# The way back of the 48-point stage: four frequencies in three packed matrix products

## The chip, the cores and the metric

One core of a Trainium2 chip runs one program. The metric is the device time of the program in microseconds (us), as the median of the runs shown. Engines: TensorE (PE; its weight loads PEld), VectorE (DVE), ScalarE (ACT), GpSimd (POOL), SyncE (SP, which here issues nearly all DMAs).

## The reference

The first half is a long convolution of 8 sequences (B = 8, S = 5696, D = 128) with one filter, along the sequence, by a real Fourier transform of length 2S. The second half is a mixture of experts with one expert of eight for each of the 45568 tokens:

```python
Xf = np.fft.rfft(x, n=L, axis=1); Hf = np.fft.rfft(h, n=L, axis=0)
y = np.fft.irfft(Xf * Hf[None], n=L, axis=1)[:, :S, :]
...
logits = x @ w_gate
expert_idx = np.argmax(logits, axis=1)
...
    h = np.maximum(xe @ w1[e], 0.0)
    ye = h @ w2[e]
    out[mask] = gate_w[mask, None] * ye
```

All inputs and outputs are float32.

## The kernel before

The transform of length 2 x 48 x 119 is cut into a 119-point stage and a 48-point stage. The batch is cut into three groups of 2, 3 and 3 sequences (`SPLIT`, line 40). For each group there are three phases. Phase A (`steps_a`, line 285) is the 119-point stage and writes its spectrum to memory in device DRAM. Phase B (`phase_b`, line 458) reads it by frequency, q = 0 to 119, transforms 48 points, multiplies with the filter's spectrum, transforms 48 points back and writes to DRAM. Phase C (`phase_c`, line 728) does the way back of the 119-point stage, finds each token's expert, and scatters the tokens, sorted by expert, to DRAM. A pipeline of expert tiles of 256 tokens (`pipeline`, line 1332) runs beside the later phases: an expert step is a quarter of a tile, first layer (`layer1`, line 1211), relu (line 1224) and second layer (`layer2`, line 1240).

The program order of every engine is written by hand: `run` (line 1418) merges streams (the phases, the preparation of expert weights, the expert pipeline) by costs that each stream yields. Phase B yields 0.45 of an expert step for a frequency of group 1 and 0.85 for group 2 (`MIX_B`, line 53, used in line 669); the preparation of weights (`weights`, line 258) is a third stream that lies beside group 1. Engines work through their own queues in that order and wait for each other by semaphores.

In phase B of groups 1 and 2 a step n treats one frequency of 3 x 128 = 384 columns (QW = 1); four frequencies (QB = 4, a block) share one load and one store. In step n, in this order:

- loads are issued for blocks to come: `load_m`, `load` (lines 631 to 634)
- stores that are `HOLD` = 3 steps old are issued on SP (line 645)
- `forward(n)`, line 537: one product of 96 rows with a 96 x 128 matrix into a bank of PSUM (tag `cx`, 4 banks in turn)
- `inverse(n - 4)`, line 574: one product of the 128 rows of `zt` with a 128 x 96 matrix (line 581) into the next `cx` bank, of which 96 partitions are used
- `product(n - 1)`, line 548: three VectorE operations (lines 557, 562, 564) that read the forward product's bank and write `zt` and `xs`
- `combine(n - 2)`, line 569: a sum on POOL (line 572; while the last sorts of group 2 run, on VectorE)
- `save(n - 5)`, line 590: ScalarE copies 96 partitions of the bank to `vt` (line 596); after the fourth, one store of the block is queued

The lags 1, 2, 4 and 5 are `BLAGS` (line 38). `zt` has 4 - 1 + 2 = 5 buffers (line 553). Each float32 product shows in the trace as two matmul records with a weight load each. The expert step of tiles 18 and later (`PLAIN`) works in split precision: six records for each of the two layers, and a remainder that VectorE forms (line 1234). Before that tile a layer has four float32 records and no remainder; the remainder of the weights is formed by VectorE in the preparation (line 279).

Column strips are in use before: `logit` (line 815) places products of 32 result rows side by side with `tile_position` (line 819), and `synth` in groups 1 and 2 puts two of 64 rows side by side (line 780). A table of tiles is made by `tables` (line 1029), which takes a `cx` bank too (line 1086); the guest is phase A of the next group, run inside phase C two halves a step (`Guest`, line 359, called in line 951).

Of the kernel before, what the change touches and what calls it, by code (L numbers as in the profile page):

```python
# [13 lines left out]
F32 = mybir.dt.float32  # L14
# [9 lines left out]
NB = 48  # L24
MB = 119
QN = 2 * 60
MP = 128
HQ = 60
HM = 64
# [12 lines left out]
SIX = 4  # L42
# [20 lines left out]
HOLD = 3  # L63
# [16 lines left out]
def conv_moe(ctx: ExitStack, tc: tile.TileContext, I, out, B, S, D, E, F, split):  # L80
    nc = tc.nc
    P = 128
    K2 = 2 * NB
# [6 lines left out]
    def pool(name, bufs, space=None):  # L90
        kw = {} if space is None else {"space": space}
        return ctx.enter_context(tc.tile_pool(name=name, bufs=bufs, **kw))
# [4 lines left out]
    ps = pool("ps", 2, PSUM)  # L97
# [15 lines left out]
    sb = Space()  # L113
# [21 lines left out]
    class Group:  # L135
        def __init__(self, g, b0, nb):
# [13 lines left out]
            self.qb = 4 if self.cols <= 384 else (3 if self.cols <= 512 else 2)  # L150
            rows = dram.tile([2 * QN + 2 * PR, NB, self.cols], F32, name=f"VU{g}")
            self.U = [rows[2 * QN + k * PR : 2 * QN + (k + 1) * PR] for k in range(2)]
            self.V = rows
# [4 lines left out]
    for g, nb in enumerate(split):  # L158
        gr = Group(g, b0, nb)
        gr.parts = []  # L160
        for upto in HALVES[g]:
            rows = sum(MB - (i + (MB - 1) * NB >= S) for i in range(upto * gr.ni))
            sure = max(0, (b0 * S + nb * rows - E * (T - 1) + T - 1) // T)
            tiles = (total if b0 + nb == B and upto * gr.ni == NB else sure) - done
# [6 lines left out]
    def by_frequency(gr, q, count, out):  # L171
        lo = 2 * (q % HQ)
        if out:
            rows = gr.V[2 * q : 2 * (q + count)]
        else:
            rows = gr.U[q // HQ][lo : lo + 2 * count]
        return rows.rearrange("(q c) i x -> (c i) q x", c=2)

    for pt in parts[:-1]:
        pt.filled = True  # L180
    HS = dram.tile([QN // 4, NB, 2, 4, D], F32, name="HS")
    WD = dram.tile([4, E * P, F], F32, name="WD")

    fcs = const.tile([MP, 3, PR], F32, name="c_fcs")
    nc.sync.dma_start(fcs, I["fcs"])
    half = fcs[:, 2]
    uht = sb.tile([K2, QN, D], F32, tag="uht", name="uht", bufs=1)
    sb.open("a")
    fcr = const.tile([MP, 2, 2, PR], F32R, name="fcr")
    nc.vector.tensor_copy(fcr[:, 0], fcs[:, :2])  # L190
# [14 lines left out]

    gcs = part_of(2 * MP, QN).rearrange("p (k m) -> p k m", k=2)
    wg = part_of(32)
    wt9 = part_of(2 * E1, MP).rearrange("p (c e) -> p c e", c=2)
    where = part_of(NB * B, MP).bitcast(I32).rearrange("p (i b) -> p i b", b=B)
    base0 = part_of(E1)  # L210
    lane = part_of(2).bitcast(I32)
    lt = part_of(MP // 2, MP).bitcast(BF16)
    upto = part_of(E * E, E)
# [188 lines left out]
    def phase_h():  # L402
# [26 lines left out]
        for n in range(nd + 2):  # L429
            cut(n + 1)  # L430
            if n < nd:
                hc = hcs.pop(n).rearrange("p v i d -> p v (i d)")
                for c in range(2):
                    banks[c] = ps.tile([P, 512], F32, tag="mh", name=f"ph{n}_{c}", bufs=2)
                    for k, (u, v) in enumerate(PASSES):
                        nc.tensor.matmul(
                            banks[c][:QN, : NB * W], fcr[:, u, c, :QN], hc[:, v], start=(k == 0), stop=(k == 2)
                        )
# [19 lines left out]
    def phase_b(gr, guest=None):  # L458
        g, cb, cw, nch, QB, QW = gr.g, gr.cb, gr.cw, gr.nch, gr.qb, gr.qw
        dp, dc, di, ds_ = BLAGS[g]  # L460
        tiles, outs_ = {}, {}
# [36 lines left out]

        mats, hhs, hbank = {}, {}, {}
        zts, banks, late, clock = {}, {}, [], [0]  # L500

        def back(qb):
            if g or qb * QB >= QN:
# [44 lines left out]
        def product(n):  # L548
            q, c = items[n]
            qb, k0 = divmod(q, QB)  # L550
            hh = hhs[qb]
            xs = sb.tile([P, cb, QW * D], F32, tag="xs", name=f"xs{g}_{q}_{c}", bufs=dc - dp + 2)
            zt = sb.tile([P, cb, QW * D], F32, tag="zt", name=f"zt{g}_{q}_{c}", bufs=di - dp + 2)
            x3 = banks.pop(n)[:, : QW * cw].rearrange("p (b x) -> p b x", b=cb)
            hv = hh[:, :, k0 : k0 + QW].rearrange("p c j (o d) -> p c o (j d)", o=1)
            wide = [cb, QW * D]
            nc.vector.tensor_tensor(out=zt, in0=x3, in1=hv[:, 0].broadcast_to([P] + wide), op=ALU.mult)  # L557
            for k in range(2):
                at, to = slice(k * HP, (k + 1) * HP), slice((1 - k) * HP, (2 - k) * HP)
                him = hv[at, 1].broadcast_to([HP] + wide)  # L560
                if k == 0:
                    nc.vector.tensor_tensor(out=xs[to], in0=x3[at], in1=him, op=ALU.mult)  # L562
                else:
                    nc.vector.scalar_tensor_tensor(  # L564
                        out=xs[to], in0=x3[at], scalar=-1.0, in1=him, op0=ALU.mult, op1=ALU.mult
                    )
            zts[n] = (zt, xs)
# [6 lines left out]
        def inverse(n):  # L574
# [12 lines left out]
                )  # L587
            banks[n] = vp

        def save(n):  # L590
            q, c = items[n]
            qb, k0 = divmod(q, QB)
            if k0 == 0 and c == 0:
                outs_[qb] = sb.tile([K2, QB, gr.cols], F32, tag="six", name=f"vt{g}_{q}", bufs=SIX)
            dst = outs_[qb][:, k0 : k0 + QW, c * cw : (c + 1) * cw]
            nc.scalar.copy(dst, banks.pop(n)[:K2, : QW * cw].rearrange("p (j x) -> p j x", x=cw))  # L596
            if k0 + QW == QB and c == nch - 1:
                late.append((clock[0], by_frequency(gr, qb * QB, QB, True), outs_.pop(qb)))
                tiles.pop(qb), hhs.pop(qb), mats.pop(qb)

        items = [(q, c) for q in range(0, QN, QW) for c in range(nch)]
        per = QB // QW * nch
        N = len(items)
        deep = 4 if g == 0 else 2
# [20 lines left out]
                filt(qb, k)  # L625
        for m in range(4 if g == 0 else 0):
            filt_save(0, m)
        for n in range(N + ds_ + 2 + (HOLD if QW == 1 else 0)):
            qb, k0 = divmod(n, per)
            clock[0] = n  # L630
            if k0 == (0 if g == 0 else 1):
                load_m(qb + deep)
            if k0 == (0 if g == 0 else min(3, per - 1)):
                load(qb + 2)
            if g == 0:
                if n < N:
                    forward(n)
                for k in range(QB // per):
                    filt(qb + 2, k0 * (QB // per) + k)
                for m in range(4 // per):  # L640
                    filt_save(qb + 1, k0 * (4 // per) + m)
                if k0 == 0:
                    back(qb)
            while late and late[0][0] <= n - (HOLD if QW == 1 else 1):
                nc.sync.dma_start(*late.pop(0)[1:])
            if n < N and g:
                forward(n)
            if 0 <= n - di < N:
                inverse(n - di)
            if 0 <= n - dp < N:  # L650
                product(n - dp)
            if 0 <= n - dc < N:
                combine(n - dc)
            if 0 <= n - ds_ < N:
                save(n - ds_)
                while late and g == 0 and n >= N:
                    nc.sync.dma_start(*late.pop(0)[1:])
            if k0 == 0:
                back_save(qb)
            if k0 == (0 if per == 1 else per - 1):  # L660
                twin(qb + 1)
            if n == 0:
                twin(0)
            drained = guest if n >= N + di - 1 and g in GUESTED else None
            if n == N - 4 and g in FETCHED and guest:
                guest.fetch()
            if drained:
                drained.begin(2)
            yield max(cw * 7 / 2.4 + 200, 2 * cw / 0.96 + 300) * QW if g == 0 else STEP * MIX_B[g]
            if drained:  # L670
                drained.end()

    lanes = []
    state = {"w9": [const.tile([MP, max(SLOTS), E1], F32, name=f"w9{k}") for k in range(2)]}
    state["ex"] = [const.tile([MP, max(SLOTS), E1], F32, name=f"ex{k}") for k in range(2)]
    state["oh"] = [const.tile([MP, max(SLOTS) + 1, E1], BF16, name=f"oh{k}") for k in range(3)]
    state["base"] = base0
    state |= {"wide": False, "alone": True, "prepped": False, "defer": False, "spare": False, "now": 0, "acting": False, "brief": 2}

    sorts = []  # L680
    scratch = [fcs[:, 0, :w] for w in WIDTHS]
# [46 lines left out]
    def phase_c(gr, guest=None, after=None):  # L728
        g, nb, cb, cw, NI, ns = gr.g, gr.nb, gr.scb, gr.scw, gr.ni, gr.ns
# [26 lines left out]
        banks = {"mh": 2, "mx": 1, "ma": 1}  # L756
# [183 lines left out]
        for n in range(n_end + 1):  # L940
            for k in range(nsub):
                at = n * nsub + k
# [5 lines left out]
                scored = k == 0 and n >= sl  # L948
                if guest:
                    few = n < QUIET[g] or scored and not state["alone"] and g  # L950
                    carried = guest.begin(1 if few else 2)
                if n < nu:
                    made = synth(n, k)
                if TL <= at < total_sub + LL:
# [3 lines left out]
                whole = 0 <= at - LL < total_sub and (at - LL) % nsub == nsub - 1  # L958
                if whole:
                    for j in range(nsub):  # L960
                        spare = tp if j else ybank.get((n, k))
                        if spare is None:
                            spare = bank(f"lp{g}_{n}_{k}", "mh")
# [65 lines left out]
    def tables(pt, base):  # L1029
        g, NT = pt.s, pt.nt  # L1030
# [28 lines left out]
        start = sb.tile([E, E + 1], F32, tag="start", name=f"start{g}", bufs=1)  # L1059
# [26 lines left out]
        bank = ps.tile([P, 512], F32, tag="cx", name=f"tb{g}", bufs=4)  # L1086
        at = bank[:1, : 2 * NT]
        nc.tensor.matmul(at, unit, ge.rearrange("p c j -> p (c j)"), start=True, stop=True)
        yield LATER
        tab = const.tile([1, 3, NT], I32, name=f"tab{g}")  # L1090
        jr = jrow[0:1, :NT]
        r0 = sb.tile([1, NT], F32, tag="r0", name=f"r0{g}", bufs=1)
# [454 lines left out]
```

## Time and profile before

| | |
|---|---|
| median of 3 runs | 2096.18 us (2093.4 to 2098.55) |
| profiled execution, its own time | 2100.94 us |
| its span, first to last instruction | 2099.2 us |
| mean granted TensorE clock | 0.985 of 2.4 GHz |
| busy: PE, DVE, ACT, POOL | 2024.5, 1469.1, 1060.5, 1207.0 us |
| chain that ended last, by engine | PE 46%, issue 14%, POOL 8%, DMA 5% |
| phase B of group 1 | in the stretch from 390 to 656 us |
| phase B of group 2 | in the stretch from 921 to 1258 us |

Busy time is the union of an engine's instructions. Matmul records overlap: the next product starts before the record of the last one ends, so the distance between starts tells what a product costs. A wait names the engine that waited, what it wanted to run, and what ended the wait.

### The profile page before, as it was taken

What the parts mean: (1) busy time and instruction counts of PE and PEld (TensorE: products, weight loads), DVE (VectorE), ACT (ScalarE), POOL (GpSimd) and SP (SyncE); (2) the same over time, 40 slices, a digit from 0 to 9 for tenths busy, and PEclk for the clock granted to TensorE, in tenths of its full rate; (3) what the DMA queues carried; (4) which work ended last, traced back from release to release, by engine and by line L of the source; (5) the groups of instructions that cost most, each with busy time, mean ns of one, the idle gap of its engine ahead of it and who ended that gap; (6) DMA issues with size and microseconds to landing.
All of it is one profiled execution on the core that took longest, in us unless ns stands there. A gap on an engine that the chain in (4) does not pass through costs nothing.

```text
span 2099.2 us, 45580 instructions
## 1 busy us (share of the span) xinstructions
PE 2024.5 (96%) x13868; PEld 1624.7 (77%) x13868; DVE 1469.1 (70%) x3179; ACT 1060.5 (51%) x2291; POOL 1207.0 (57%) x1370
## 2 busy tenths in 40 slices
PE   8999898899999999989999999999999999999998
PEld 4788454566666666667777778888899999999998
DVE  5788565588885787778887886777765555555554
ACT  3688453355554545534544544555544554554554
POOL 1366277566563588865655661888874444444443
PEclk9999999999999999999999999999999999999999
DMA  8899998899998889778877786666565443444441
GB/s 275 280 288 302 311 356 295 228 292 299 297 287 290 283 295 313 269 187 226 230 214 217 226 243 224 221 218 223 189 213 181 147 147 112 132 133 138 135 143 35
DMA packets 239942, 477.24 MB, mean 227 GB/s; under 512 B 33202, under 2 KB 145847, under 8 KB 239696
## 3 DMA queue, kind: packets, MB, share of 16 engines
q1 hardware_dynamic: 215328, 426.01, 65.1%
q0 software_dynamic: 24368, 48.29, 6.8%
q8 instruction: 113, 1.85, 0.4%
q14 instruction: 133, 1.09, 0.2%
HBM read 567.76 MB, written 178.26 MB: 355 GB/s over the span
## 4 chain that ended last, share of the span: by engine, by line
PE 46%; issue 14%; POOL 8%; DMA 5%; DVE 2%; ACT 1%; POOLq 0%; SPq 0%; DVEq 0%
PE mh L1221 11%; PE ma L1253 11%; POOL out L1308 8%; PE vp L581 5%; PE xp L545 5%; DMA wb<-WD 4%; PE yp L780 3%; PE tp L196 2%; PE mx L196 2%; PE pa L313 2%; PE ma L1248 2%; PE mh L1218 1%; PE yp L819 1%; PE tp L819 0%; PE gb L196 0%
## 5 line engine op out<-in xcount | busy, mean ns | idle before, releaser
L1234 DVE SCALAR_TENSOR_TENSOR hs<-mh,hs 128x512 fp32r<-128x512 f32 x656 | 451.2, 688 | 375.5 <-ACT hs L1232 370.1
L1221 PE MATMUL mh<-xtb,wb 128*128 128x256 f32 x3936 | 609.5, 291 | 15.1 <-DMA wb<-WD 8.8
L1232 ACT ACTIVATE hs<-mh 128x512 fp32r<-128x512 f32 x656 | 392.2, 598 | 438.8 <-PE mh L1221 431.4
L1253 PE MATMUL ma<-hs,wb 128*128 128x256 f32 x3936 | 589.4, 285 | 8.3 <-DMA wb<-WD 8.3
L1221 PEld LDWEIGHTS mh<-xtb,wb 128*128 128x128 f32 x3936 | 519.5, 190 | 60.6 <-issue 27.9
L693 POOL DMA_INDIRECT SR<-rt,pi x384 | 387.8, 1010 | 236.4 <-ACT ev L324 82.0
L1253 PEld LDWEIGHTS ma<-hs,wb 128*128 128x128 f32 x3936 | 511.0, 190 | 9.8 <-DMA wb<-WD 9.7
L1308 POOL DMA_INDIRECT out<-xr x252 | 247.5, 982 | 296.9 <-DVE xr L1271 247.0
L572 POOL TENSOR_TENSOR zt<-zt,xs 128x384 f32<-128x384 f32 (+1 forms) x294 | 315.1, 1085 | 133.8 <-DVE xs L564 107.8
L596 ACT COPY vt<-vp 96x384 f32<-96x384 f32 (+1 forms) x300 | 148.9, 497 | 278.8 <-PE vp L581 271.9
L545 PE MATMUL xp<-uq,mt 96*128 96x384 f32 (+1 forms) x720 | 257.5, 452 | 4.4 <-DMA uq<-VU 3.5
L581 PE MATMUL vp<-zt,mi 128*96 128x384 f32 (+1 forms) x720 | 257.5, 453 | 3.4 <-DVE xs L564 1.7
L557 DVE TENSOR_TENSOR zt<-xp,hh 128x384 f32<-128x384 f32 (+1 forms) x300 | 174.3, 581 | 70.7 <-PE xp L545 61.6
L327 DVE TENSOR_TENSOR ut<-ev,pa 128x512 f32<-128x512 f32 x192 | 122.9, 681 | 108.8 <-ACT ev L324 92.0
L1308 POOL DMA_INDIRECT out<-xb x112 | 109.3, 976 | 133.5 <-ACT hs L1232 97.6
L564 DVE SCALAR_TENSOR_TENSOR xs<-xp,hh 64x384 f32<-64x384 f32 (+1 forms) x300 | 175.9, 586 | 6.0
L581 PEld LDWEIGHTS vp<-zt,mi 128*96 128x96 f32 x720 | 112.0, 163 | 86.4 <-issue 42.0
L562 DVE TENSOR_TENSOR xs<-xp,hh 64x384 f32<-64x384 f32 (+1 forms) x300 | 173.3, 578 | 6.0
L545 PEld LDWEIGHTS xp<-uq,mt 96*128 96x128 f32 x720 | 129.3, 191 | 41.0 <-issue 13.2
L313 PE MATMUL pa<-xt,c_fcs 64*128 64x512 f32 x384 | 119.4, 659 | 3.0 <-DVE ut L327 2.3
L687 POOL TENSOR_TENSOR c_fcs<-c_fcs 128x64 f32<-128x64 f32 (+1 forms) x288 | 115.4, 401 | 2.1
L769 DVE TENSOR_TENSOR vr<-vq 120x384 f32<-120x384 f32 x192 | 108.8, 608 | 0.4 <-DMA vq<-VU 0.4
(138 smaller groups left out, 2178.5 us busy)
## 6 DMA issues: line engine op xcount, KB each, us to landing
wb<-WD SPq DMA_DIRECT2D x656, 512.0 KB
vq<-VU SPq DMA_DIRECT2D x128, 384.0 KB
VU<-ut SPq DMA_DIRECT2D x48, 768.0 KB
uq<-VU SPq DMA_DIRECT2D x60, 576.0 KB
VU<-vt SPq DMA_DIRECT2D x60, 576.0 KB
xt<-x SPq DMA_DIRECT2D x96, 256.0 KB
xr<-SR SPq DMA_DIRECT2D x182, 130.0 KB
wf<-moe_w SPq DMA_DIRECT2D x72, 256.0 KB
```

The lines of the kernel that those rows point to most:

```text
L545: nc.tensor.matmul(xj, mt[:, k0 + j, :], uc.rearrange("p (b d) -> p b d", d=D), start=True, stop=True)
L557: nc.vector.tensor_tensor(out=zt, in0=x3, in1=hv[:, 0].broadcast_to([P] + wide), op=ALU.mult)
L562: nc.vector.tensor_tensor(out=xs[to], in0=x3[at], in1=him, op=ALU.mult)
L564: nc.vector.scalar_tensor_tensor(out=xs[to], in0=x3[at], scalar=-1.0, in1=him, op0=ALU.mult, op1=ALU.mult)
L572: eng.tensor_tensor(out=zt, in0=zt, in1=xs, op=ALU.add)
L581: nc.tensor.matmul(vp[:K2, j * cw : (j + 1) * cw].rearrange("p (b d) -> p b d", d=D), mi[:, k0 + j, :], zt.rearrange("p b (j d) -> p b j d ...
L693: s = nc.gpsimd.indirect_dma_start(out=SR[:, :], out_offset=IndirectOffsetOnAxis(ap=pi[:, b : b + 1], axis=0), in_=rt[:, b, :], in_offset= ...
L1221: nc.tensor.matmul(hp[:, u, :], wb[:, a, f, :], xt[:, b, :], start=(n == 0), stop=(n == 2))
L1232: done = nc.scalar.activation(hs[:, 0], hp, AF.Relu)
L1234: nc.vector.scalar_tensor_tensor(out=hs[:, 1], in0=hp, scalar=0.0, in1=hs[:, 0].bitcast(F32), op0=ALU.max, op1=ALU.subtract)
L1253: nc.tensor.matmul(accs[t], wb[:, a, f, :], hs[:, b, u, :], start=(k == 0 and u == 0 and n == 0), stop=(k == NPAIR - 1 and u == 1 and n == 2),
L1308: sc = nc.gpsimd.indirect_dma_start(out=out[:, :], out_offset=IndirectOffsetOnAxis(ap=xr[:, s, D + 1 : D + 2].bitcast(I32), axis=0), in_=x ...
```

## The change

The matrix of a way back has 96 columns, so 32 of the array's 128 columns are free. In groups 1 and 2 the way back of a block of four frequencies is done at once, in three products of 128 result rows. Product j holds frequency j in column strips 0 to 2 and a third of the fourth frequency (its rows 32j to 32j + 31) in strip 3. Every strip is a matmul of its own, with 32 columns of weights and 384 columns of data, so a block has 12 matmuls where it had four.

The burst stands in the step in which the block's last frequency used to go back (step n with n - 4 its index). In that step `forward(n)` is left out; it comes first in the next step, before `forward(n + 1)`. ScalarE copies three banks of 128 partitions, the first in the step of the burst, the two others in the next. A block leaves in two stores: 96 partitions x 3 rows, and 32 partitions x 3 rows. `zt` gets a sixth buffer. The stage runs three steps longer at its end, in which only stores are issued. While a table's bank is held, the guest does not begin a half (`tight`).

```diff
+STRIP = 32
...
+        packed = QW == 1
...
-            zt = sb.tile([P, cb, QW * D], F32, tag="zt", name=f"zt{g}_{q}_{c}", bufs=di - dp + 2)
+            zt = sb.tile([P, cb, QW * D], F32, tag="zt", name=f"zt{g}_{q}_{c}", bufs=di - dp + (3 if packed else 2))
...
+        def inverse_packed(qb):
+            mi = tiles[qb][1]
+            for j in range(QB - 1):
+                vp = ps.tile([P, 512], F32, tag="cx", name=f"vq{g}_{qb}_{j}", bufs=4)
+                for at in range(0, P, STRIP):
+                    k, lo = (j, at) if at < K2 else (QB - 1, j * STRIP)
+                    nc.tensor.matmul(
+                        vp[at : at + STRIP, :cw].rearrange("p (b d) -> p b d", d=D),
+                        mi[:, k, lo : lo + STRIP],
+                        zts[qb * QB + k][0],
+                        start=True,
+                        stop=True,
+                        tile_position=(0, at),
+                    )
+                banks["v", j] = vp
+            for k in range(QB):
+                zts.pop(qb * QB + k)
+
+        def save_packed(qb, j):
+            if j == 0:
+                outs_[qb] = sb.tile([P, QB - 1, gr.cols], F32, tag="six", name=f"vt{g}_{qb}", bufs=SIX)
+            nc.scalar.copy(outs_[qb][:, j], banks.pop(("v", j))[:, :cw])
+            if j == QB - 2:
+                q, vt = qb * QB, outs_.pop(qb)
+                late.append((clock[0], by_frequency(gr, q, QB - 1, True), vt[:K2]))
+                one = gr.V[2 * q + 2 * (QB - 1) : 2 * q + 2 * QB].rearrange("c i x -> (c i) x")
+                late.append((clock[0], one.rearrange("(j r) x -> r j x", r=STRIP), vt[K2:]))
+                tiles.pop(qb), hhs.pop(qb), mats.pop(qb)
...
-        for n in range(N + ds_ + 2 + (HOLD if QW == 1 else 0)):
+        for n in range(N + ds_ + 2 + (HOLD + QB - 1 if packed else 0)):
...
-            if n < N and g:
+            whole, rest_of = divmod(n - di - QB + 1, QB)
+            burst = packed and rest_of == 0 and 0 <= whole < N // QB
+            if packed and rest_of == 1 and 0 <= whole and n <= N:
+                forward(n - 1)
+            if n < N and g and not burst:
                 forward(n)
-            if 0 <= n - di < N:
+            if burst:
+                inverse_packed(whole)
+            if not packed and 0 <= n - di < N:
                 inverse(n - di)
             if 0 <= n - dp < N:
                 product(n - dp)
             if 0 <= n - dc < N:
                 combine(n - dc)
-            if 0 <= n - ds_ < N:
+            if burst:
+                save_packed(whole, 0)
+            if packed and rest_of == 1 and 0 <= whole < N // QB:
+                for j in range(1, QB - 1):
+                    save_packed(whole, j)
+            if not packed and 0 <= n - ds_ < N:
                 save(n - ds_)
...
-                    carried = guest.begin(1 if few else 2)
+                    carried = guest.begin(0 if state["tight"] else 1 if few else 2)
...
         nc.tensor.matmul(at, unit, ge.rearrange("p c j -> p (c j)"), start=True, stop=True)
+        state["tight"] = True
         yield LATER
+        state["tight"] = False
```

## Rows read from the trace of the kernel before

**Rows 1.** Stretches: length, busy PE PEld DVE ACT POOL, clock, DMA share, GB/s.

```profile
390.00:656.00 266.00, 260.77 (x976) 171.70 (x975) 228.26 (x395) 131.89 (x253) 163.38 (x159) 1.00 1.01 291
921.00:1258.00 337.00, 324.82 (x1850) 249.30 (x1850) 287.29 (x538) 162.69 (x307) 197.08 (x201) 0.98 0.79 223
```

**Rows 2.** Timeline of TensorE in group 1's stage: start us, us, engine, line, operation, tiles.

```profile
439.19 0.81 PE L545 MATMUL xp<-uq,mt 96*128 96x384 f32 x2
439.83 0.81 PE L581 MATMUL vp<-zt,mi 128*96 128x384 f32 x2
440.48 1.02 PE L1218 MATMUL mh<-xtb,wf 128*128 128x256 f32 x4
...
442.21 0.81 PE L545 MATMUL xp<-uq,mt 96*128 96x384 f32 x2
```

**Rows 3.** Waits, 390 to 656 us: who waited for whom, us, times, longest.

```profile
ACT vt L596 <- PE vp L581: 128.6, 81, 4.0
...
DVE zt L557 <- PE xp L545: 26.4, 20, 14.0
...
PEld vp L581 <- POOL zt L572: 6.2, 9, 1.4
...
PE vp L581 <- DVE xs L564: 1.7, 3, 0.8
```

**Rows 4.** Waits, 921 to 1258 us.

```profile
DVE zt L557 <- PE xp L545: 23.4, 20, 4.4
...
PE ma L1253 <- DMA wb<-WD: 4.9, 4, 2.9
PEld mh L1221 <- DVE xs L564: 4.7, 10, 3.2
PEld mh L1221 <- DVE hs L1234: 3.4, 9, 2.1
```

**Rows 5.** Timeline of TensorE beside two and three column strips, in group 2's phase C.

```profile
1299.94 0.87 PE L1221 MATMUL mh<-xtb,wb 128*128 128x256 f32 x6
...
1300.65 0.87 PE L1253 MATMUL ma<-hs,wb 128*128 128x256 f32 x6
...
1301.45 0.87 PE L780 MATMUL yp<-vr,c_small 120*64 120x384 f32 x4
...
1302.24 0.55 PE L196 MATMUL tp<-ident,rt 128*128 128x128 f32 x3
...
1302.72 0.42 PE L819 MATMUL yp<-yt,c_small 128*32 128x128 f32 x6
...
1302.96 0.39 PE L819 MATMUL tp<-yt,c_small 128*32 128x128 f32 x6
```

**Rows 6.** Timeline in group 1's stage: VectorE's products, and one that waited for TensorE.

```profile
439.23 0.56 DVE L557 TENSOR_TENSOR zt<-xp,hh 128x384 f32<-128x384 f32 x1
...
440.96 0.56 DVE L557 TENSOR_TENSOR zt<-xp,hh 128x384 f32<-128x384 f32 x1
...
446.96 0.81 PE L545 MATMUL xp<-uq,mt 96*128 96x384 f32 x2
...
447.81 0.56 DVE L557 TENSOR_TENSOR zt<-xp,hh 128x384 f32<-128x384 f32 x1 [0.55 <-PE xp L545]
```

**Rows 7.** Groups by line, 390 to 656 us: count | busy us, mean ns | idle before.

```profile
L596 ACT COPY vt<-vp 96x384 f32<-96x384 f32 x119 | 56.6, 475 | 129.5 <-PE vp L581 128.6
...
L1228 ACT ACTIVATE hf<-mh 128x512 f32<-128x512 f32 x56 | 33.4, 596 | 3.9 <-PE mh L1218 3.6
...
L279 DVE TENSOR_TENSOR wsp<-wraw,wsp 128x512 fp32r<-128x512 f32 x22 | 23.8, 1080 | 4.4 <-ACT wsp L277 3.8
```

**Rows 8.** Groups by line, 921 to 1258 us.

```profile
L1234 DVE SCALAR_TENSOR_TENSOR hs<-mh,hs 128x512 fp32r<-128x512 f32 x106 | 73.3, 692 | 21.3 <-ACT hs L1232 18.2
...
L1209 DVE TENSOR_TENSOR xtb<-mx,xtb 128x256 fp32r<-128x256 f32 x27 | 11.2, 414 | 0.0
```

**Rows 9.** Timeline in group 2's stage: SP issues a store of a block.

```profile
959.63 0.37 SPq L645 DMA_DIRECT2D VU<-vt  x1
```

More of the change, by code (lines that the diff above doesn't have):

```diff
@@ L601, in phase_b @@
         items = [(q, c) for q in range(0, QN, QW) for c in range(nch)]
+        assert not packed or QB == 4 and nch == 1
         per = QB // QW * nch
@@ L677, in conv_moe @@
     state["base"] = base0
-    state |= {"wide": False, "alone": True, "prepped": False, "defer": False, "spare": False, "now": 0, "acting": False, "brief": 2}
+    state |= {"wide": False, "alone": True, "prepped": False, "defer": False, "spare": False, "now": 0, "tight": False, "acting": False, "brief": 2}
     sorts = []
```

## The prediction

> **What bounds the kernel now.** I read the time by stretches first. The change lives in two stages, the ways through the 48-point stage of groups 1 (390 to 656 us) and 2 (921 to 1258 us). In both TensorE is busy for 98 and 96% of the time, VectorE for 86 and 85%, ScalarE for half, at a granted clock of 0.98 or more (2.4 GHz) [rows 1]. A busy TensorE need not stream at its peak, so I looked next at the starts of its products in the timeline. A forward product starts, the way back starts 0.65 us later, the next one again 0.64 or 0.65 us later, and an expert step (both layers) takes 1.73 us to the next start [rows 2]. A frequency without an expert step thus takes 1.29 us. Waits in group 1's stage are small: the way back waited 6.2 us for POOL and 1.7 us for VectorE [rows 3]. In group 2's stage the experts' first layer waited for VectorE 4.7 and 3.4 us, the second 4.9 us for weights [rows 4]. So TensorE sets the end of both stages, and what is taken from its queue counts, unless a wait takes its place. VectorE is close behind: that is the reader's point to watch.
>
> **What TensorE gives back.** Four ways back take 4 x 0.65 = 2.59 us now. After the change they are one burst of three products, each of four column strips, two matmul passes a strip. No row of before has four strips, so I bound it by neighbours [rows 5]. Two strips of 384 columns, from a second layer to the transposes: the layer lasts 0.80 us to the strips' start where the layer before it lasted 0.71 (0.09 to enter), the strips 0.79 where one whole product takes 0.65 (0.14 to leave). Three strips of 128 columns start 0.24 us before the next three; a third of 0.65 is 0.22, so three abreast cost 0.02 more than one. At best a packed product costs 0.65; by the three-strip rows' ratio 0.72; if only two strips ran abreast, 1.30. I take 0.66, near the strip rows, as the extra 0.02 looks like issue time of the strips and not like slower streaming. Burst: 0.09 + 3 x 0.66 + 0.14 = 2.21, with 0.06 for the first load behind it that can't be fetched ahead, 2.28. Saved: 0.31 us in each of 60 rounds, **18.6 us**. Ends: 0.35 (21 us) and, at 0.72, 0.13 (8 us).
>
> The Trainium skill ("TensorE: Matmul & The Clock Gate", Part 3, measured speedup) speaks against this: it gives three column strips 2.38 times one, not 3. A packed product would then be 0.65 x 3 / 2.38 = 0.82 us by estimate, the burst 2.75, and the 18.6 us saved would be about 10 us lost. The 0.24 us of [rows 5] bears that out only in part.
>
> **What the new order costs.** This decides. A round of four frequencies now is: burst; two forward products F1, F2 in the next step; F3; F4; burst. VectorE's products P1 to P4 follow one step behind; one takes 1.73 us or, start to start without a gap, about 1.71 [rows 6]. Three new ties appear, all from the text of the change.
> (a) F1 is issued in the step in which P1 is issued, so VectorE has no stock of work: P1 begins when F1 ends, 0.04 us after the record's end [rows 6].
> (b) The third packed product takes the bank of F3, so it needs P3 done.
> (c) P4 writes the buffer that the first packed product reads, so it waits for that; and the next F1 takes the bank of F4, so it waits for P4. Behind a waiting P4 stand the relu remainders and weight splits of VectorE; behind a waiting F1 or strip stands all of TensorE, F2 and the expert steps first.
>
> Set time 0 at the start of F2; F1's record ends at 0.16. VectorE: P1 0.20 to 1.91, P2 to 3.62, P3 to 5.33.
> Group 1, expert steps in every second gap (56 in 120 [rows 7]; the planner's share is 0.45). **Order one**, experts behind the burst and behind F3: F2 to 0.65, F3 1.30, expert 3.03, F4 3.68, packed products at 3.77, 4.43 and due at 5.09, but P3 frees the bank at 5.33 + 0.06: 0.3 us lost. P1's sum on POOL ends about 1.91 + 0.15 + 1.0 = 3.1, so the burst finds it done unless a scatter stands before it.
> **Order two**, experts behind F2 and F4: the burst starts at 5.41, the first packed product ends at 6.32 by its record, P4 runs 6.36 to 8.07; TensorE is ready for F1 at 7.6 and waits until 8.1: 0.5 us lost.
> **One expert step** in the round (four of 30: 26 x 2 + 4 = 56): P1 to P4 end at 7.04, F1 starts at 7.1, so the round takes 7.75 where TensorE alone would need 2.6 + 2.28 + 1.73 = 6.6: 1.1 us lost.
> Sum: 13 x 0.3 + 13 x 0.5 + 4 x 1.1 = 14.8 us. To this come the 22 weight splits on VectorE, 1.08 us each [rows 7]. Now VectorE's backlog swallows them; then one that falls before P3 in order one (half of 13 x 0.73) or anywhere in a short round (4 x 0.73) delays TensorE by its length: 8.3 us. Against it stand the old waits for POOL and VectorE, of which I credit 5 us [rows 3]. Group 1: -9.3 + 14.8 + 8.3 - 5 = **+9 us**.
>
> Group 2: an expert step behind nearly every frequency (106 in 120 [rows 8]), of two layers of 0.71 us, 1.42 [rows 5]. With four (16 rounds) VectorE has P1 to 1.91, a relu remainder of 0.69 [rows 8], P2, a remainder to 5.02, while TensorE reaches the fourth first layer, which needs that remainder's bank, at 4.8: 0.25 us. With three (14 rounds), by where the missing step was: 0.4 behind the burst, 1.0 behind F2, 0.1 behind F3, 0.5 behind F4; mean 0.5. The other VectorE work of a tile (two of 0.41 us, 27 tiles [rows 8]) delays one round in four by 0.8: 6 us. Sum 4 + 7 + 6 = 17; credit 6 of the old waits [rows 4]. Group 2: -9.3 + 17 - 6 = **+2 us**.
>
> **The other edits, each at nothing.** ScalarE makes three copies of 128 partitions for four of 96: 60 x 0.475 = 28 us less [rows 7], but it waited 128.6 us for the way back in one stage [rows 3], so no one waits for it. SP issues two stores for one, 60 x 0.37 = 22 us of its queue [rows 9], with the same 384 packets of 1.5 KB (288 + 96); loads behind them are issued two rounds ahead. If SP were late, forward products would wait for their rows; I allow up to 5 us. The skipped guest step beside a table moves a transform by one step, four times, and takes nothing away; it can shift by its 1 us each, so 4 us at most. Three more empty steps at the end of a stage are filled by expert steps that would come later anyway. One more buffer and the flag cost no time.
>
> **Sum.** The profiled execution took 2100.94 us (span 2099.2), 4.8 over the median of the runs, 2096.18; the changes count from either alike. +9 + 2 = +11: 2112 for an execution like the profiled one, **2107 us** as a median.
>
> **Rivals.**
> *The gain comes through.* For it: TensorE is the bound, its queue is shorter by 18.6 us, and VectorE, on the whole 14% idle [rows 1], would catch up in the wider gaps. Against: ties (a) to (c) empty its backlog once a round. It needs expert steps that fall behind the burst and splits that fall behind P3, so that a round loses under 0.1: -18.6 to -8, 2078 to 2088. Chance 0.21.
> *It evens out.* As forecast, but half of the stalls were there before in another name or the splits fall well: -6 to +6, 2090 to 2102. Chance 0.27.
> *The strips hinder one another.* What I read as leaving the strips is slower streaming, and a packed product takes the 0.79 us of [rows 5]: burst 0.09 + 3 x 0.79 + 0.06 = 2.52, 0.24 more than above, 14 us: 2121. For it: no row shows four strips at once. Against: three strips at 0.24 us. Chance 0.07. The Trainium skill's figure above would have it so, and worse.
> *The change does not do what it says*: only two strips abreast; burst 0.29 + 3 x 1.30 = 4.2, 1.9 us over mine in 60 rounds, +115: 2222. Chance 0.03; two abreast is all that the 384-column rows show.
> *Forecast, stalls outweigh the gain*, +6 to +20: chance 0.42.
>
> About 0.3% (6.3 us) is what a measurement of this kernel can tell from no change. Faster 0.21; within 0.27; slower 0.42 + 0.07 + 0.03 = 0.52. The range reaches from most of the gain, 2080, to the forecast's stalls with no credit (11 us) and part of the hindered strips, 2126; outside lie the pairs, the rest of the hindered strips and the very end of the gain, 0.1 to 0.15. The likeliest case alone: 2102 to 2116.
>
> **What would show it.** In the profile after: twelve matmuls of 32 columns (24 records) a round, a burst of 2.2 to 2.3 us from its start to the next line's; passes of four strips about 0.32 us apart. Forward products that wait for VectorE (the third read of P4) once in about two rounds of group 1, some 0.5 us; strips that wait for it at the third packed product; VectorE idle for forward products in every round, so well over the 26 and 23 us that it waits now [rows 3, 4]. Group 1's stage about 9 us longer, group 2's about equal, ScalarE 28 us less busy. The forecast is wrong if TensorE's waits for VectorE in the two stages stay under 15 us together (then it is faster), or if passes of four strips lie over 0.4 us apart (then far slower).

## The result and the profile after

The changed kernel takes 2124.01 us (median of 4 runs, 2121.1 to 2128.49) against 2095.27 us beside it (4 runs, 2093.4 to 2098.55): a ratio of 1.0119, 95% interval 1.0098 to 1.0141. By the ratio it is slower by about 25 us (the two medians lie 28.7 us apart) where +11 was forecast; the direction and the range held, the size did not. The profiled execution took 2128.49 us at a mean granted clock of 0.984.

The head of the page, its chain by engine, and the lines of the new burst (line 598) and its copies (line 613):

```profile
span 2126.6 us, 47386 instructions
...
PE 2022.8 (95%) x14828; PEld 1583.7 (74%) x14828; DVE 1471.8 (69%) x3179; ACT 1027.8 (48%) x2231; POOL 1207.7 (57%) x1370
...
PE 32%; issue 16%; POOL 11%; DMA 4%; DVE 3%; ACT 1%; POOLq 1%; SPq 1%; DVEq 0%; ACTq 0%
...
L613 ACT COPY vt<-vq 128x384 f32<-128x384 f32 x180 | 81.0, 486 | 242.4 <-PE vq L598 224.2
...
L598 PE MATMUL vq<-zt,mi 128*32 128x384 f32 x1440 | 135.6, 493 | 7.5 <-DVE xs L566 7.2
```

The burst is there as planned: 1440 records are 60 rounds of 24, and ScalarE works 1027.8 us, 32.7 less than before (28 forecast). TensorE's busy time barely moved, though it got less to do; so I looked at the two stages, by the windows view (columns as in [rows 1]):

```profile
395.00:670.00 275.00, 258.99 (x1465) 151.79 (x1466) 227.97 (x395) 118.19 (x223) 161.80 (x158) 0.99 0.96 277
939.00:1282.00 343.00, 324.73 (x2328) 229.21 (x2329) 290.07 (x538) 145.05 (x279) 199.55 (x205) 0.98 0.79 221
```

TensorE's share fell from 98 to 94% in group 1's stage, from 96 to 95% in group 2's, at a granted clock of 0.99 and 0.98 of 2.4 GHz: it waits more. For whom, the waits say. Of group 1's stage, 395 to 670 us:

```profile
DVE zt L559 <- PE xp L547: 24.2, 19, 4.3
...
PEld vq L598 <- DVE xs L566: 15.8, 19, 1.8
PEld xp L547 <- DVE xs L566: 15.5, 21, 1.8
...
PEld xp L547 <- ACT vt L613: 8.6, 13, 1.4
...
DVE zt L559 <- PE vq L598: 7.9, 11, 1.3
PEld vq L598 <- POOL zt L574: 6.5, 12, 0.8
PE vq L598 <- DVE xs L566: 6.3, 9, 1.1
...
PE xp L547 <- DVE xs L566: 5.0, 6, 1.2
```

Of group 2's stage, 939 to 1282 us:

```profile
PEld mh L1266 <- issue: 30.3, 40, 3.2
...
DVE zt L559 <- PE xp L547: 18.2, 23, 1.7
PEld mh L1266 <- DVE hs L1279: 12.5, 16, 1.8
...
DVE zt L559 <- PE vq L598: 11.0, 12, 4.1
```

Rows that begin with PE give idle time of the matmuls themselves: before, the way back waited 1.7 us for VectorE in group 1's stage [rows 3]; now strips wait 6.3 and forward products 5.0 us. The rows of weight loads (PEld), 15.8 and 15.5 us, also hold idle time that costs nothing, as the next timeline shows. In group 2's stage it is the experts' first layer, which stands in TensorE's queue behind whatever waits, and whose weight loads' wait for relu's remainder grew from 3.4 [rows 4] to 12.5 us (8.0 in another execution of the kernel before).

One round of group 1 in the timeline (start, length, engine):

```profile
452.85 2.14 PE L598 MATMUL vq<-zt,mi 128*32 128x384 f32 x24
...
454.92 0.30 PEld L547 LDWEIGHTS xp<-uq,mt 96*128 96x128 f32 x2 [0.62 <-ACT vt L613]
454.92 1.56 PE L547 MATMUL xp<-uq,mt 96*128 96x384 f32 x4
...
457.63 0.69 DVE L280 TENSOR_TENSOR wsp<-wraw,wsp 128x512 fp32r<-128x512 f32 x1
...
459.43 1.53 PE L598 MATMUL vq<-zt,mi 128*32 128x384 f32 x16
...
461.22 0.56 DVE L566 SCALAR_TENSOR_TENSOR xs<-xp,hh 64x384 f32<-64x384 f32 x1
...
461.83 0.85 PE L598 MATMUL vq<-zt,mi 128*32 128x384 f32 x8 [0.87 <-DVE xs L566]
```

The first burst runs through: the next line's start is 2.07 us later, as behind every burst that runs through. The load of that line is listed with 0.62 us of idle time which a copy of ScalarE ended. That is no wait: idle time of 0.62 us or more stands before the load behind each of the 60 bursts, whatever engine is named. In the next burst, a weight split (457.63, 0.69 us) has delayed VectorE, so the third packed product waits 0.87 us for the bank that the round's third frequency frees at 461.78. This is tie (b) with a split before it, as the prediction described it.

Finally the stages by their first and last starts in the trace. I count as wait what a stage holds beyond its products at their undisturbed distances, that is from start to start where nothing waits ([rows 2], and 2.16 us for a burst).

| us | before | after | difference |
|---|---|---|---|
| group 1's stage | 262.6 (waits 6.7) | 274.0 (28.3) | +11.4 |
| from there to phase C | 16.2 | 23.4 | +7.2 |
| phase C of group 1 | 215.7 | 213.6 | -2.1 |
| group 2's stage | 336.1 (21.5) | 341.9 (39.7) | +5.8 |
| from there to phase C | 20.0 | 23.4 | +3.4 |
| all the rest | 1248.6 | 1250.3 | +1.7 |

The stages hold 17 of 27 us (about 2 of them one expert step more in group 1's, 56 where there were 55). Another 10.6 lie behind them, where no way back is packed: one expert step more behind group 1's, two behind group 2's, and this wait of the sort behind group 1's stage (waits, 669 to 694 us):

```profile
PE mx L197 <- DMA xr<-SR: 3.5, 1, 3.5
```

This made the small edits suspect.

### The profile page after: what moved, and what is told of

Same layout as the page of the kernel before. It is cut to its first block, busy times and chain, and to the rows that moved or that the text cites. A ratio compares the mean times of both kernels' runs of the same rounds, so it can differ in the third digit from the quotient of the medians.

```text
span 2126.6 us, 47386 instructions
## 1 busy us (share of the span) xinstructions
PE 2022.8 (95%) x14828; PEld 1583.7 (74%) x14828; DVE 1471.8 (69%) x3179; ACT 1027.8 (48%) x2231; POOL 1207.7 (57%) x1370
## 4 chain that ended last, share of the span: by engine, by line
PE 32%; issue 16%; POOL 11%; DMA 4%; DVE 3%; ACT 1%; POOLq 1%; SPq 1%; DVEq 0%; ACTq 0%
PE mh L1266 9%; PE ma L1298 8%; POOL out L1353 8%; PE yp L823 3%; PE xp L547 3%; PE vq L598 2%; POOL SR L736 2%; DMA wb<-WD 2%; PE tp L197 2%; PE mx L197 1%; PE pa L314 1%; POOL c_fcs L730 1%; DMA SR<-rt,pi 1%; DVE hs L1279 1%; PE yp L862 1%
## 5 line engine op out<-in xcount | busy, mean ns | idle before, releaser
L1266 PE MATMUL mh<-xtb,wb 128*128 128x256 f32 x3936 | 599.6, 288 | 23.4 <-DMA wb<-WD 10.8
L547 PE MATMUL xp<-uq,mt 96*128 96x384 f32 (+1 forms) x720 | 248.3, 458 | 13.3 <-DMA uq<-VU 6.6
L613 ACT COPY vt<-vq 128x384 f32<-128x384 f32 x180 | 81.0, 486 | 242.4 <-PE vq L598 224.2
L598 PE MATMUL vq<-zt,mi 128*32 128x384 f32 x1440 | 135.6, 493 | 7.5 <-DVE xs L566 7.2
L598 PEld LDWEIGHTS vq<-zt,mi 128*32 128x32 f32 x1440 | 38.8, 109 | 82.2 <-issue 43.6
```

Source lines behind the costliest of these rows:

```text
L547: nc.tensor.matmul(xj, mt[:, k0 + j, :], uc.rearrange("p (b d) -> p b d", d=D), start=True, stop=True)
L598: nc.tensor.matmul(vp[at : at + STRIP, :cw].rearrange("p (b d) -> p b d", d=D), mi[:, k, lo : lo + STRIP], zts[qb * QB + k][0], start=True ...
L1266: nc.tensor.matmul(hp[:, u, :], wb[:, a, f, :], xt[:, b, :], start=(n == 0), stop=(n == 2))
```

## The experiments

Each ratio is to the kernel before on the same chip, with its 95% interval. The chips differ (the kernel before has medians of 2095 to 2158 us), so only ratios are compared. Stage lengths come from one profiled execution each; the kernel before gave 336.1 and 330.1 us for group 2's stage on two, so a few us there show nothing.

**Is VectorE the wall? (missed its aim.)** In groups 1 and 2 the product does two of its three operations, in the kernel before and in the changed one:

```diff
-            for k in range(2):
+            for k in range(1 if QW == 1 else 2):
...
-            eng.tensor_tensor(out=zt, in0=zt, in1=xs, op=ALU.add)
+            lo = HP if QW == 1 else 0
+            eng.tensor_tensor(out=zt[lo:], in0=zt[lo:], in1=xs[lo:], op=ALU.add)
```

> The kernel before, with VectorE's third operation of a product left out in groups 1 and 2 (one half of the sum on POOL with it), so a VectorE product takes 1.14 us in place of 1.71. Theory (VectorE's chain decides only in the new order): TensorE still sets the end, 2082 to 2093 us. Rival (VectorE was the bound before as well): 2060 or less. It is the partner of the next run.

> The changed kernel with the same VectorE operation left out. Theory: four products take 4.6 us of VectorE, so the ties to the third bank and to the buffer are met in time, and the burst's 0.35 us a round shows: 8 to 20 us less than the kernel before without that operation. Rival one (strips or their mode cost more than the trace's starts tell): as much slower against its partner as the full pair is, +20 to +30 us. Rival two (empty steps and the skipped guest steps make most of the loss): between -8 and +5 against its partner.

Measured: 1.1161 (1.1124 to 1.1199) and 1.1274 (1.1235 to 1.1313). Less work took 12 to 13% longer. Phase B's waits in the first of them (420 to 760 us) show where:

```profile
DVE xs L562 <- POOL zt L573: 123.6, 34, 6.8
...
POOL zt L573 <- DMA out<-xr: 69.5, 18, 7.2
PE vp L582 <- POOL zt L573: 64.0, 27, 4.6
POOL zt L573 <- DMA SR<-rt,pi: 37.7, 9, 6.3
```

VectorE and TensorE wait for POOL's sum, and the sum waits until a scatter of tokens has landed. In the kernel before, a sum starts right behind a scatter; here it starts 5 us later (POOL's timeline, two lines of the kernel before, two of this run):

```profile
509.89 0.99 POOL L1308 DMA_INDIRECT out<-xr  x1 [3.02 <-DVE xr L1271]
510.90 1.97 POOL L572 TENSOR_TENSOR zt<-zt,xs 128x384 f32<-128x384 f32 x2
...
503.54 0.99 POOL L1309 DMA_INDIRECT out<-xr  x1 [0.28 <-POOL zt L573]
509.48 5.77 POOL L573 TENSOR_TENSOR zt<-zt,xs 64x384 f32<-64x384 f32 x6 [4.95 <-DMA out<-xr]
```

By the semaphores in the trace, 110 of the 294 sums on POOL wait so for the scatter issued just before them, with 387 us of idle time; before, none does. The edit put a tie on POOL that neither kernel has (why is not shown). It also changes the convolution and with it the tokens' experts: 668 remainders of expert steps were formed (line 1235), 656 before. So the pair says nothing about VectorE.

**Which part costs?** First tie (c) alone: one more buffer for `zt` in the changed kernel.

```diff
-bufs=di - dp + (3 if packed else 2)
+bufs=di - dp + (4 if packed else 2)
```

> The changed kernel with a seventh zt buffer, so the fourth VectorE product no longer waits for the first packed product; nothing else. Theory: the waits of the second expert order in group 1 (13 rounds of 0.5 us) and of the rounds of group 2 without an expert step behind the burst go, 6 to 10 us less than the changed kernel, 2114 to 2118 us. Rival (the third packed product's bank is what binds): within 3 us of the changed kernel.

Measured 1.0099 (1.007 to 1.0129), within the interval of the change itself. By the ratios the tie is worth about 4 us (0.2%; 3 us beside the changed kernel on the same chip, below), if anything. VectorE's waits for strips, 7.9 and 11.0 us in the two stages, are gone from its list, but those for forward products rise from 24.2 to 30.9 and from 18.2 to 23.7 us: most of the idle time came back under another name.

Then the packing without the three empty steps and without the skipped halves; the unchanged kernel before as a ruler; and the two side edits in the kernel before, without any packing:

```diff
-        for n in range(N + ds_ + 2 + (HOLD + QB - 1 if packed else 0)):
+        for n in range(N + ds_ + 2 + (HOLD if packed else 0)):
...
-                    carried = guest.begin(0 if state["tight"] else 1 if few else 2)
+                    carried = guest.begin(1 if few else 2)
```

> The changed kernel without the three empty steps at a stage's end and without the guest's skipped halves. Theory: the ties inside the rounds are the loss, and these two edits only 3 to 7 us of it: 2117 to 2121 us. Rival (they are most of it, by the expert steps that they move): 2105 to 2112. Forecast's own step (they cost nothing): within 2 us of the changed kernel.

> The kernel before, unchanged, for its trace on the same chip as the next three. Every theory: the way through the 48-point stage takes about 263 us in group 1 and 336 us in group 2, as before.

> The kernel before with the two side edits alone: three more empty steps at the end of the stage in groups 1 and 2, and the guest's skipped halves; no packing. Theory (the side edits only shift the expert steps against the rounds, and the shift hurts because the packed rounds have no slack): within 4 us of the kernel before. Rival (the side edits cost by themselves, 16 to 20 us of the changed kernel's loss): +12 to +20 us. Forecast's own step: 0.

> The changed kernel without the three empty steps, the guest's skipped halves kept. If the empty steps are the part of the side edits that costs: as the kernel with packing only, 1.002 to 1.006 times the kernel before. If the skipped halves cost: as the changed kernel, 1.009 to 1.013.

> The kernel before with the guest's skipped halves alone (no packing, no empty steps). If the skipped halves are what costs in the side edits: 1.005 to 1.008 times the kernel before, with the load of sorted rows that a late tile waits for behind group 1's stage. If the empty steps are: 0.999 to 1.002.

`e7_no_steps` is the changed kernel without the empty steps, `e9_skip_only` the kernel before with the skipped halves. The side edits alone and the changed kernel without empty steps were run again, beside the changed kernel:

> The changed kernel once more, on the same chip as the next two. Theory: 1.009 to 1.014; its distance to the kernel without empty steps (last of this call) is what the empty steps cost.

> The kernel before with empty steps and skipped halves, no packing, once more. If the empty steps cost by themselves: 1.005 to 1.009. If the first look was a chance of that chip: 0.998 to 1.003.

> The changed kernel without its empty steps, skipped halves kept, once more. If the empty steps cost 0.5% or more: 1.003 to 1.006, at least 0.004 under the changed kernel of this call. If the sum is made by the skipped halves: 1.008 or more.

| kernel | ratio | group 1's stage (waits) | behind it | group 2's stage (waits) |
|---|---|---|---|---|
| before again | 2094.27 us (one run) | 262.6 (6.7) | 16.2 | 330.1 (15.5) |
| changed, again | 1.0112 (1.0083 to 1.0142) | 268.5 (22.8) | 24.6 | 342.1 (39.9) |
| packing only | 1.004 (1.0016 to 1.0064) | 264.6 (21.1) | 16.4 | 336.7 (34.5) |
| side edits only | 1.0067 (1.0046 to 1.0088) | 271.6 (13.5) | 24.5 | 339.2 (24.6) |
| side edits only, again | 1.0052 (1.0032 to 1.0072) | 267.9 (9.8) | 24.1 | 339.9 (25.3) |
| skipped halves only | 1.0013 (0.9992 to 1.0034) | 269.7 (11.7) | 21.5 | 330.9 (16.3) |
| changed, no empty steps | 1.004 (1.0022 to 1.0058) | 270.3 (24.7) | 22.3 | 334.4 (32.2) |
| the same again | 1.0073 (1.0045 to 1.01) | 268.6 (22.9) | 21.2 | 335.6 (33.4) |

The packing alone costs 0.3 to 0.4%, 7 to 9 us (1.0031 when run again, below); the side edits alone, which add no work at all, cost 0.5 to 0.7%, 11 to 14 us. Of the side edits, the skipped halves bring one more expert step into group 1's stage (56 where there were 55) and lengthen the stretch behind it by 5 us; the wait for the sorted rows appears with the side edits and no packing (664 to 690 us):

```profile
PE mx L196 <- DMA xr<-SR: 3.5, 1, 3.5
```

But by the whole time that is given back in later phases: 0.13%, not to be told from nothing. So it is the empty steps that make the difference in the kernel before. In the changed kernel their removal gave 1.004 on one chip and 1.0073 beside 1.0112 on another, where the intervals overlap. They issue nothing of their own, yet each yields its share to the planner, and every expert step behind them changes place.

**Can the packing's own waits be loosened?** Three tries, all on the packing alone. One keeps the forward product of the burst's step ahead of the burst (with one more `zt` buffer); one puts the weights' remainders, VectorE's 22 splits, on POOL, with a control in the kernel before; one puts the expert steps where the prediction's arithmetic wants them.

```diff
-            if packed and rest_of == 1 and 0 <= whole and n <= N:
-                forward(n - 1)
-            if n < N and g and not burst:
+            if n < N and g:
```

> Packing without the side edits, with a seventh zt buffer and the forward product of the burst's step kept in its own step, ahead of the burst. The first VectorE product of a round then has its bank a step earlier, and the fourth no longer waits for the burst. Theory: the ties that empty VectorE's backlog are gone but for the third bank, so stalls in group 1's stage fall from 21 to under 14 us and in group 2's to under 28, and the kernel is 4 to 14 us faster than the kernel before (0.993 to 0.998). Rival (the order of the forward products doesn't matter): 1.002 to 1.006, as with packing only.

```diff
-                rest_of = nc.gpsimd if n < SOON else nc.vector
+                rest_of = nc.gpsimd
```

> Packing without the side edits once more, on the same chip as its partners here. Theory: in-round waits of some 16 us in group 1's stage and 15 in group 2's against 12 us of matrix time given back in each: 1.002 to 1.006 times the kernel before, group 1's stage 1 to 5 us longer, group 2's 0 to 5.

> Packing without the side edits, and the weights' remainder (line 279 of the kernel before, 22 operations of 1.08 us in group 1's stage) on POOL in place of VectorE. Theory (VectorE's chain is what the packed rounds wait for): 5 to 10 us less than packing only in group 1's stage, 0.996 to 1.001 times the kernel before. Rival (banks or POOL's sums bind, not VectorE): the same as packing only or slower, 1.003 or more.

> The kernel before with the same operation on POOL: the control of the run above. Theory: VectorE's backlog swallowed it, so within 3 us of the kernel before (0.9985 to 1.0015). Rival (VectorE bound there too): 4 us or more faster.

```diff
+PLACE = (None, (0.495, 0.495, 0.005, 0.005), (0.3, 0.27, 0.23, 0.2))
```

Here a step of phase B yields four times `MIX_B[g]`, times the entry of `PLACE` for its place in the round, with one more `zt` buffer.

> Packing without the side edits, a seventh zt buffer, and the stage's planned cost laid on other steps of a round: none behind the burst and behind the fourth forward product, half behind the first two and half behind the third (group 2: 0.2, 0.3, 0.27 and 0.23 of a round). In group 1 both expert steps of a round then lie between forward products, where VectorE needs the time. Theory (the waits come from where expert steps fall against the three ties): by the sums of the prediction the third bank is free 1.4 us early and the fourth product doesn't wait for the burst, so group 1's in-round waits fall from 22 to under 12 us, its stage to 250 to 258 us, group 2's to 325 to 334, 0.991 to 0.998 of the kernel before. Rival (VectorE or the banks bind on the average over a round, whatever the order): 1.001 to 1.006 as with packing only.

| kernel | ratio | group 1's stage (waits) |
|---|---|---|
| packing again | 1.0031 (1.0013 to 1.005) | 266.2 (22.7) |
| forward product first | 1.0056 (1.0034 to 1.0078) | 269.4 (25.9) |
| splits on POOL | 1.0024 (1.0003 to 1.0046) | 264.9 (21.4) |
| control: splits on POOL, not packed | 1.0006 (0.9984 to 1.0028) | 264.0 (8.1) |
| planned order | 1.0047 (1.0024 to 1.0071) | 270.0 (24.3) |

No try helped beyond its interval. Group 2's stage took 337.0, 341.1, 340.6, 341.5 and 332.5 us in this order; the control, which isn't packed, took the longest, so these single executions rank nothing there. Waits of the packing alone (405 to 680 us):

```profile
PEld vq L598 <- DVE xs L566: 12.1, 20, 1.6
PEld xp L547 <- DVE xs L566: 10.3, 20, 1.8
...
PEld vq L598 <- POOL zt L574: 8.6, 13, 1.6
PEld xp L547 <- ACT vt L613: 8.5, 13, 1.0
```

The same with the splits on POOL:

```profile
PEld xp L547 <- DVE xs L566: 8.8, 18, 1.8
PEld xp L547 <- ACT vt L613: 8.4, 14, 1.0
...
PEld vq L598 <- DVE xs L566: 7.1, 13, 1.0
```

And with the planned order (405 to 690 us):

```profile
PEld xp L548 <- ACT vt L614: 14.0, 23, 0.6
...
PEld xp L548 <- DVE xs L567: 9.3, 11, 1.4
PEld vq L599 <- DVE xs L567: 8.7, 11, 1.7
```

With the splits gone the strips' loads wait 5 us less for VectorE, so the splits are in it, but the stage is only 1.3 us shorter and the ratio 0.0007 lower, where the prediction had 8.3 us. With the experts in place, strips and forward products wait for VectorE 11 times each where it was 20, but by these rows not much less in sum: 8.7 and 9.3 us, where it was 12.1 and 10.3. The rows for ScalarE's copies are no tie: 22 of the 23 in the planned order, and 11 of the 13 with the packing alone, are the 0.62 us behind a burst, with the next start as early as behind any other burst. Keeping the forward product ahead moves the waits into the burst: 17.7 of its 25.9 us lie between the packed products, 11.2 at the third (with the packing alone 11.2 and 4.7).

**Which empty steps?** The changed kernel with them behind group 1's stage only, and behind group 2's only:

```diff
-(HOLD + QB - 1 if packed else 0)
+(HOLD + (QB - 1 if g == 1 else 0) if packed else 0)
```

> The changed kernel with the three empty steps in group 1's stage alone. They shift the expert steps of group 2's stage against its rounds: six rounds there then have the missing expert step behind the two forward products, so three forward products stand in a row. Theory: that place costs about 1 us a round, 6 us: group 2's stage takes 339 to 344 us, as in the full change, and the kernel 1.009 to 1.013 times the kernel before. Rival (the empty steps cost where they stand): half of the distance between the full change and the kernel without them.

> The changed kernel with the three empty steps in group 2's stage alone, behind which no packed stage follows. Theory: as without empty steps, 1.003 to 1.008 times the kernel before, group 2's stage 333 to 337 us, at least 0.003 under its partner. Rival as above.

Measured: 1.0077 (1.0054 to 1.01) and 1.0029 (1.001 to 1.0047), whose intervals don't meet. So the three behind group 1's stage cost more than those behind group 2's, by about 0.5%. That the latter cost nothing is not shown: the kernel without any was not run on this chip (1.004 and 1.0073 on others), and the kernel with the former alone lies below the full change (1.0119 and 1.0112), if within the intervals.

In all kernels with empty steps behind group 1's stage and packing, the missing expert step of six rounds of group 2 falls behind the two forward products, so that three forward products stand in a row. Group 2's stage then has 38.5 to 40.4 us of waits. Packed kernels without the empty steps have 32.2 to 34.8, but 38.9 with the forward product first, 38.4 with the splits on POOL and 30.3 in the planned order; the second kernel here has 40.7 us without that pattern, in a profiled execution 9 us over its median. Part of this spread is the wait for the experts' weights. Group 2's stage in the first and in the second kernel here:

```profile
PE mh L1266 <- DVE hs L1279: 5.2, 8, 1.1
...
PE mh L1266 <- DMA wb<-WD: 3.6, 3, 2.9
...
PE ma L1298 <- DMA wb<-WD: 0.5, 1, 0.5
```

```profile
PE ma L1298 <- DMA wb<-WD: 9.0, 5, 3.0
...
PE mh L1266 <- DVE hs L1279: 3.5, 6, 1.0
...
PE mh L1266 <- DMA wb<-WD: 1.2, 1, 1.2
```

The experts' first layer waits 5.2 to 7.1 us for relu's remainder in the kernels with the pattern and 2.2 to 4.6 us in the packed ones without it. That speaks for the pattern, with 2 to 4 us. So it is shown on one chip which empty steps cost more; the place where they do so is not shown.

## What the prediction had right, and the step that failed

**What TensorE gives back: right, a little better than forecast.** Of the 300 distances between passes inside the 60 bursts 271 are 0.322 to 0.347 us, as for a whole product; the others are longer, up to 1.60 us where a strip waits. A burst that runs through takes 2.07 us to the next start and 0.09 to enter, 2.16 where 2.28 was forecast. The forecast's 0.06 for the first load behind it stands in no row; with that load in it, the next start lies 0.44 us behind the last pass, so leaving costs 0.11, where 0.14 + 0.06 was taken. Against four ways back of 0.643 us that is 0.41 us a round, or 12.4 us a stage, where 9.3 was forecast. The waits in the tables are counted with these distances, so they hold no second measurement of it. *Two abreast* and *the strips hinder one another* are out.

By the Trainium skill's 2.38 for three column strips ("TensorE: Matmul & The Clock Gate", Part 3, measured speedup) a packed product was estimated at 0.82 us. The trace does not agree: four strips took 0.64 to 0.67 us for the two passes of a product, and three strips of 128 columns took 0.24 us where a third of a whole product takes 0.22 [rows 5].

**What the new order costs: right in kind and near in size.** Packing alone raises the waits of group 1's stage from 6.7 to 21 to 23, that is by 14 to 16 (forecast 14.8 + 8.3 - 5 = 18), and group 2's from 15.5 or 21.5 to 34.5, by 13 to 19 (forecast 11). Less 12.4 each, that makes about +3 and +4, 7 us, and the runs say 7 to 9. The parts were less well sized, so the near sum is partly luck: the gain was larger, the splits count about 1 us and not 8.3, and tie (c) some 4 us if anything. Which waits make up the rest is shown only in part.

**VectorE's idleness: half right.** I expected it to idle for forward products well over 26 and 23 us, in every round. It idled 24.2 and 18.2, in 19 and 23 places, and 7.9 and 11.0 more for the strips (tie (c)). But more than half of the 26.4 us before lies ahead of the stage's first product:

```profile
393.81 0.56 DVE L557 TENSOR_TENSOR zt<-xp,hh 128x384 f32<-128x384 f32 x1 [14.03 <-PE xp L545]
```

After the change 4.3 us lie there. Inside the rounds of group 1 it is 12.4 us before and 19.9 after, so there the sign came as described; in group 2 only the sum with the strips rose.

**"The other edits, each at nothing": the step that failed.** "Three more empty steps at the end of a stage are filled by expert steps that would come later anyway", says the prediction. Without any packing the side edits cost 0.5 to 0.7%, 11 to 14 us, about as much as was forecast for the whole. They are why +25 came where +11 was forecast, as packing alone makes +7 to +9. Of the two, the skipped halves (4 us allowed) cost 0.13%, not to be told from nothing, and the empty steps the rest. That expert steps are only moved is true of the work and not of the time, which here depends on where they fall. Packing (0.35%) and side edits (0.6%) add up to 0.95%; the remaining 0.2% is within the intervals. The two stores for one were rightly costed: forward products waited for their rows once in each stage, 2.2 and 3.5 us (before, 2.9 in group 1's and nothing in group 2's).

**What stays open.** By which wait the empty steps behind group 1's stage lengthen the run. A lighter VectorE that leaves POOL's waits and the tokens' experts alone was not tried, nor more than four banks. No version ran faster than the kernel before.

## What to carry to other kernels

Matrix time taken from a stage whose next engine is 86% busy comes back as waits once the results are wanted in bursts from a few banks in turn; loosening one tie gives the next its name, so count all takings of a bank in a round. A list of waits says who came last before a start, not what the start lost: compare the start with one where nothing waits. An edit that adds no work, but a step in a hand-merged order, is not free: time it alone, with the main edit left out. And an experiment that leaves work out can add a tie or change the data: look at its waits before reading its time.

## What was not expected of the hardware

Four strips of 32 columns with 384 columns of float32 data ran at the rate of one whole product, 0.322 to 0.347 us a pass, with 0.09 us to enter and 0.11 to leave. And chips differ by more than the change: the kernel before has a median of 2095 us on one and of 2141 and 2158 us on others. Of the 34 us between two profiled executions of the changed kernel on two chips, 17 are there when group 1's stage starts: phase C of group 0 took 104.8 and 127.1 us for the same program. Why is not shown.
